# A hand-frozen instruction order laid out anew, without its zero products

## The chip, the cores and the metric

The kernel runs on one core of a Trainium2 chip. The metric is the time of one execution in microseconds (us) on the device. A core has five instruction streams that run side by side and meet only at semaphores: TensorE (PE, matrix products), VectorE (DVE), ScalarE (ACT), GpSimd (POOL) and SyncE (SP, which here issues nearly all transfers). In the profile, PEld is TensorE's loading of weights.

## The reference

Two attention blocks read the same input `x` (2048 rows of 512, bf16), with 32 heads of 16 columns each. Block A is a linear attention with a learned softmax feature map; block B is ordinary softmax attention. A gate per row mixes the two.

```python
x = A_x
g = _sigmoid((x * gate_w).sum(-1, keepdims=True))
a = _A_ref(x, A_wqkv, A_w_phi, A_wo)      # q, k through w_phi, softmax(+) and softmax(-) as features
b = _B_ref(x, B_wqkv, B_wo)               # softmax(q k^T / 4) v, 2048 x 2048 scores for each of 32 heads
return g * a + (1 - g) * b
```

The scores of block B are the bulk of the work: 32 heads x 2048 x 2048 exponentials, each of which needs a product before it and one after it.

## The kernel before, in words

**Tiles.** A score tile is 128 keys x 512 queries of one head. There are 32 blocks; a block is one chunk of 512 queries for four heads, so that a block has 4 x 16 = 64 tiles. A tile is made by one product with 32 rows of TensorE (`qk_mm`, L994: four tiles with different heads can run at once, one in each quarter of the rows), its exponential is taken, and it is used by a product with 32 columns (`pv_mm`, L1136: four at once, one in each quarter of the columns), which adds into the one accumulator `psO` of the block.

**Two ways of taking the exponential.** Most tiles go to ScalarE two at a time (`add_exp`, L1115, 128x1024). `DN` gives for each block how many tiles take the other way: VectorE writes the tile as 16-bit integers whose bits are a rough exponential (`D1`, L1084), GpSimd adds constants to the same words in two steps (`shifted`, L1060), and TensorE adds up the three versions (`add_pvd`, the operations `pvdt`, `pvds` and `pvdm`). Two D1 of the same group of four can be joined into one VectorE instruction over two banks (`Plan.join`, L1074, 128x1024). 756 tiles go this way.

**Banks.** PSUM has eight banks of 512 floats. One is `psO`; the others (`psS`, numbers 0 to 6) take the score tiles (two neighbouring banks for a ScalarE pair, one for a D1 tile) and the results of all projections. A bank that an operation takes must first have been read out by whoever drained its last content.

**Everything else fills in.** The projections of q, k and v (`k_fill`, `q_fill`, `v_fill`, `v_pair`; L754, L842, L855), the whole of block A (`phi`, `kv_half`, `z_rest`, `q_rest`) and the output products (`out_tile`, `out_part`, `out_last`) are cut into short operations (`fill`) that lie between the score products. The normalization of a finished block goes through DRAM: `ev` copies `psO` (L1231), and transfers `ld`, `lq`, `mg`, `lr`, `rb` on SP carry sums and reciprocals about, until `T2` multiplies (L1247). The odd heads of a q chunk are cut out by transfers `qo` and `qe` (L897, L899).

**The order is a table.** `_build` lists 5,401 operations with their dependencies. `Plan.place` (L477) then reads `TABLE`: for each of the five engines the list of operation numbers in the order in which its stream runs them, in `pairs` the D1 that are joined, and in `homes` one digit for each operation that takes a bank (7 is `psO`). `Plan.emit` writes the streams with the semaphore waits that the dependencies need. An engine runs its list strictly in order: an operation that waits holds up everything behind it on that engine. A `-1` in TensorE's list is a filler (`Plan.filler`, L455): four products of a block of zeros with 512 columns of `xT` (`zero_mm`, L1126), added into `psO`, where they change nothing. The numbers in the constants above the table (`DN`, `PHASES`, `POOL_ADDS`, `SHIFT` and so on) fix which tiles go which way.

```python
self.order = {e: [known[k] if k >= 0 else self.filler(k) for k in table[e]] for e in ENGINES}
for op in self.order["pe"]:
    if op.acq is not None:
        op.acq.bank = homes[int(next(bank))]
for a, k in table["pairs"]:
    self.join(known[a], known[k])
```

Of the kernel before, what the change touches and what calls it, by code (L numbers as in the profile page):

```python
# [84 lines left out]
        0, 17, 2, 4, 5, 6, 7, 8, 10, 9, 11, 13, 14, 12, 15, 22, 26, 23, 27, 24, 25, 28, 29, 21, 132, 19, 967, 133, 968, 30, 20, 1094,  # L85
        1096, 1095, 1098, 139, 1099, 140, 146, 1235, 1236, 1227, 1228, 147, 1366, 1367, 1370, 1368, 1371, 1507, 1516, 1508, 1517, 1654,
        1656, 1655, 1658, 1659, 1795, 1804, 1805, 1925, 1796, 1926, 1927, 1929, 1930, 2070, 2071, 2062, 2217, 2063, 2218, 2221, 2222,
        2219, 2358, 2349, 2350, 2359, 2484, 2485, 2486, 2488, 2489, 2625, 2634, 2635, 2626, 2763, 2764, 2765, 2767, 2768, 2900, 2891,
        2901, 531, 2892, 533, 3038, 3039, 3040, 3042, 3043, 552, 32, 554, 558, 559, 3207, 555, 562, 561, 3208, 3216, 560, 31, 557, 3346,
        3347, 3348, 556, 3350, 3217, 3351, 3483, 3491, 603, 3484, 571, 574, 605, 3492, 580, 577, 3626, 3628, 3627, 581, 584, 583, 3630,  # L90
        582, 3631, 626, 624, 3803, 3811, 627, 628, 630, 633, 634, 631, 3804, 632, 3812, 3942, 629, 3943, 3946, 3642, 3944, 3652, 3947,
        4091, 675, 4100, 3662, 4101, 4092, 677, 643, 4234, 4236, 4235, 646, 649, 4238, 652, 4239, 654, 656, 696, 698, 655, 653, 4412, 704,
        699, 4403, 702, 4404, 700, 4413, 703, 705, 4542, 4543, 701, 4546, 4544, 4547, 4260, 749, 3672, 706, 747, 4708, 4709, 4270, 715,
        718, 4250, 721, 724, 4832, 727, 4833, 726, 725, 728, 4836, 4834, 4837, 770, 768, 4280, 776, 772, 777, 775, 773, 774, 5008, 771,
        4848, 778, 5009, 5139, 5140, 787, 790, 5143, 5141, 5144, 796, 793, 800, 798, 4858, 799, 4878, 797, 4868, 5396, 5399, 5400
    ),
    "act": (
        1, 16, 3, 18, 75, 87, 81, 805, 809, 910, 806, 911, 810, 918, 916, 913, 921, 933, 923, 926, 928, 931, 938, 936, 941, 943, 948, 946,
        961, 956, 953, 951, 963, 958, 971, 969, 1058, 1065, 1053, 1050, 1060, 1048, 1068, 1055, 1063, 1073, 1078, 1075, 1080, 1083, 1070,
        1088, 1085, 1171, 1101, 1090, 1186, 1103, 1178, 1176, 1188, 1173, 1191, 1181, 1183, 1196, 1193, 1201, 1203, 1198, 1208, 1211,  # L100
        1213, 1216, 1206, 1221, 1223, 1218, 1237, 255, 1239, 1320, 260, 1325, 1322, 1327, 1330, 1332, 1335, 1337, 1340, 1342, 1345, 1347,
        1350, 1352, 1355, 1357, 282, 1360, 1362, 1374, 1376, 1466, 1468, 1471, 1473, 1476, 1478, 1481, 1483, 1486, 1488, 1491, 1493, 1496,
        1498, 1501, 1503, 1509, 1518, 1608, 287, 1610, 1613, 1615, 309, 1620, 1618, 1623, 1625, 1628, 1630, 1633, 1635, 1638, 1640, 1643,
        1645, 314, 1648, 1650, 1662, 336, 1664, 1754, 1756, 1759, 1761, 1764, 1766, 1769, 1771, 1774, 1776, 240, 1779, 1781, 1784, 1786,
        1789, 1791, 341, 1797, 1806, 1874, 1876, 1879, 1881, 1884, 1886, 1889, 1891, 1894, 1896, 1899, 1901, 1904, 1906, 1909, 1911, 1914,
        1916, 1919, 1921, 1932, 1934, 2011, 2013, 2016, 2018, 2021, 2023, 2026, 2028, 2031, 2033, 2036, 2038, 2041, 2043, 2046, 2048,
        2051, 2053, 2056, 2058, 2092, 2094, 2171, 2173, 2176, 2178, 2181, 381, 2183, 386, 2186, 2188, 2191, 2193, 2196, 2198, 2201, 2203,
        2206, 2208, 2211, 2213, 2224, 2226, 2303, 2305, 2308, 2310, 2313, 408, 2315, 2318, 413, 2320, 2323, 2325, 435, 2328, 2330, 2333,
        2335, 2338, 2340, 2343, 440, 2345, 2351, 2360, 2428, 2430, 2433, 2435, 2438, 2440, 462, 2443, 2445, 2448, 2450, 2453, 2455, 2458,
        2460, 2463, 2465, 2468, 2470, 2473, 2475, 467, 2480, 2478, 2492, 2494, 2584, 2586, 517, 2589, 2591, 2594, 2596, 2599, 2601, 2604,  # L110
        2606, 2609, 2611, 2614, 2616, 2619, 2621, 2627, 2636, 2717, 2719, 2722, 2724, 2729, 2727, 2734, 2732, 2737, 2739, 2742, 2744,
        2747, 2749, 2752, 2754, 2757, 2759, 2770, 2772, 2840, 2842, 2845, 2847, 2850, 2852, 2855, 2857, 2860, 2862, 2865, 2867, 2870,
# [1550 lines left out]
```

## Time and profile before

| | |
|---|---|
| time, median of 3 runs | 660.23 us (659.39 to 660.83) |
| span of the profiled execution, first to last instruction | 657.6 us |
| busy: TensorE products / ScalarE / VectorE / GpSimd | 649.1 / 635.1 / 609.4 / 410.8 us |
| granted TensorE clock, mean | 1.000 |
| transfers, mean | 47 GB/s |

The profiled execution's own time is not given apart from the runs; its span leaves out what lies before the first and after the last instruction, and is 2.6 us less than the median. A row of a view names the line of the kernel, the engine, the operation, what it writes and reads, how often, and then busy time, mean duration in ns, and idle time of the engine before it. Line numbers are those of helpers, so that a line can stand for many operations. A product is shown with its passage through the array (some 0.38 us), and products overlap: TensorE can look busy through a short wait. The same holds for ScalarE and VectorE, whose instructions overlap by a tenth of a microsecond.

### The profile page before, as it was taken

The numbers are of one execution on the slowest core, as the hardware profiler recorded it, in microseconds if no ns is written. First come the engines' busy times: TensorE is split into PE (matmuls) and PEld (weight loads), VectorE is DVE, ScalarE is ACT, GpSimd is POOL, SyncE is SP. The second block draws the span as 40 slices with busy tenths as digits, with TensorE's granted clock in tenths as the row PEclk, the third lists the DMA queues.
The fourth block names the chain that finished last, engine by engine and source line by source line (L and its number), as shares of the span: only waits on it lengthen the run. The fifth ranks groups of instructions, "written<-read, shape, count | busy, mean of one in ns | idle before, by whom it ended". The sixth has DMA issues, their size and how long they took to land.

```text
span 657.6 us, 20651 instructions
## 1 busy us (share of the span) xinstructions
PE 649.1 (99%) x8820; PEld 227.3 (35%) x8820; DVE 609.4 (93%) x963; ACT 635.1 (97%) x720; POOL 410.8 (62%) x437
## 2 busy tenths in 40 slices
PE   8999999999999999999999999999999999999997
PEld 4333333434333333333233233322333333332333
DVE  6999899999998789999999999999999989999985
ACT  6999999999999999999999999999989999999996
POOL 7575367465665446486467876575867566656853
PEclk9999999999999999999999999999999999999999
DMA  6530101001010000000012431233211633134132
GB/s 131 104 100 12 33 12 27 11 11 19 11 27 10 16 18 8 19 17 14 23 37 47 100 77 33 63 78 68 48 51 35 102 56 83 35 63 103 44 84 48
DMA packets 67947, 30.94 MB, mean 47 GB/s; under 512 B 53208, under 2 KB 62808, under 8 KB 67856
## 3 DMA queue, kind: packets, MB, share of 16 engines
q1 hardware_dynamic: 65840, 28.82, 19.6%
q8 instruction: 69, 1.13, 0.7%
q10 hardware_dynamic: 1632, 0.79, 0.5%
q14 instruction: 22, 0.18, 0.1%
q0 software_dynamic: 384, 0.02, 0.1%
HBM read 7.87 MB, written 8.88 MB: 25 GB/s over the span
## 4 chain that ended last, share of the span: by engine, by line
PE 85%; DVE 12%; ACT 1%; issue 1%; DMA 1%; SPq 0%; DVEq 0%
PE psO L1136 32%; PE psS L994 30%; PE psS L754 15%; DVE Tx_t L1084 3%; PE psS L1417 3%; DVE Ty_t L1084 1%; DVE oT_t L1084 1%; DVE Wp_t L1084 1%; PE psS L842 1%; ACT E_t L1115 1%; DVE Tz_t L1084 1%; PE psS L1514 1%; PE psS L855 1%; PE psO L1126 1%; DMA phiK_t<-in_A_x_dram 1%
## 5 line engine op out<-in xcount | busy, mean ns | idle before, releaser
L1115 ACT ACTIVATE E_t<-psS 128x1024 bf16<-128x1024 f32 x643 | 601.9, 1068 | 11.2 <-PE psS L994 10.3
L994 PE MATMUL psS<-qz_t,kTB_t 32*128 32x512 bf16 (+1 forms) x2054 | 267.5, 383 | 2.8 <-ACT E_t L1104 0.6
L1084 DVE TENSOR_SCALAR Tx_t<-psS 128x512 int16<-128x512 f32 x246 | 163.2, 682 | 10.5 <-PE psS L994 9.4
L994 PEld LDWEIGHTS psS<-qz_t,kTB_t 32*128 32x128 bf16 x2054 | 71.8, 91 | 226.4 <-ACT E_t L1115 102.9
L1136 PE MATMUL psO<-E_t,vaug_t 128*32 128x512 bf16 x1292 | 119.0, 384 | 0.0
L1060 POOL INT64_ADD vA_t<-vA_t x72 | 71.6, 999 | 19.0 <-PE psO L1136 13.7
L1084 DVE TENSOR_SCALAR Ty_t<-psS 128x512 int16<-128x512 f32 x114 | 76.5, 682 | 4.8 <-PE psS L994 4.5
L1060 POOL INT64_ADD Ty_t<-Ty_t x42 | 44.0, 1048 | 18.5 <-PE psO L1136 18.1
L1060 POOL INT64_ADD Ty_t<-Tx_t x29 | 30.1, 1038 | 39.0 <-DVE Tx_t L1084 32.7
L1136 PE MATMUL psO<-vA_t,vaug_t 128*32 128x512 bf16 (+1 forms) x520 | 52.6, 384 | 0.0
L1136 PE MATMUL psO<-Ty_t,vaug_t 128*32 128x512 bf16 x440 | 45.4, 384 | 0.0
L1136 PEld LDWEIGHTS psO<-E_t,vaug_t 128*32 128x32 bf16 x1292 | 30.2, 95 | 39.5 <-issue 28.4
L1084 DVE TENSOR_SCALAR oT_t<-psS 128x512 int16<-128x512 f32 x62 | 41.7, 682 | 1.5 <-PE psS L994 1.0
L1084 DVE TENSOR_SCALAR Tz_t<-psS 128x512 int16<-128x512 f32 x60 | 40.2, 680 | 2.1 <-PE psS L994 1.8
L1060 POOL INT64_ADD vA_t<-Tx_t x22 | 22.7, 1032 | 31.0 <-DVE Tx_t L1084 24.1
L1060 POOL INT64_ADD phiQT_t<-Tx_t x19 | 18.9, 993 | 29.1 <-DVE Tx_t L1084 28.0
L1084 DVE TENSOR_SCALAR vA_t<-psS 128x512 int16<-128x512 f32 x54 | 36.2, 682 | 0.7 <-PE psS L994 0.3
L1084 DVE TENSOR_SCALAR WAT_t<-psS 128x512 int16<-128x512 f32 x52 | 35.2, 682 | 1.4 <-PE psS L994 1.2
L754 PE MATMUL psS<-Wp_t,xT_t 128*32 128x512 bf16 x512 | 35.8, 382 | 0.0
L754 PE MATMUL psS<-xT_t,WB_t 128*32 128x512 bf16 x480 | 34.9, 382 | 0.2
L1084 DVE TENSOR_SCALAR Wp_t<-psS 128x512 int16<-128x512 f32 x50 | 33.8, 683 | 0.9 <-PE psS L994 0.7
L1060 POOL INT64_ADD WoB_t<-oT_t x19 | 19.3, 1016 | 20.7 <-DVE oT_t L1084 16.5
(165 smaller groups left out, 920.1 us busy)
## 6 DMA issues: line engine op xcount, KB each, us to landing
dpq<-EA_t SPq DMA_DIRECT2D x16, 256.0 KB, 2.3
Rb_t<-lr SPq DMA_DIRECT2D x120, 32.0 KB, 1.9
dpo<-kv_t SPq DMA_DIRECT2D x16, 128.0 KB, 1.8
qz_t<-qz_t SPq DMA_DIRECT2D x120, 16.0 KB, 1.8
Tf_t<-Tf_t SPq DMA_DIRECT2D x60, 32.0 KB, 2.0
WB_t<-in_B_wqkv_dram SPq DMA_DIRECT2D x3, 384.0 KB, 3.6
out_dram<-WvA_t SPq DMA_DIRECT2D x8, 128.0 KB, 2.0
out_dram<-WB_t SPq DMA_DIRECT2D x6, 128.0 KB, 2.0
```

The lines of the kernel that those rows point to most:

```text
L754: ins = e.matmul(out[32 * i:32 * i + 32, :], lhsT=lhsT[:, 32 * i:32 * i + 32], rhs=rhs, start=start, stop=stop, tile_position=(0, 32 * i))
L842: mms = [lambda e, ap, i=i, t=t: e.matmul(ap[:, 128 * i:128 * (i + 1)], lhsT=xT[:, t, NQ * c + 128 * i:NQ * c + 128 * (i + 1)], rhs=W_B[:, ...
L855: mms = [lambda e, ap, i=i, t=t: e.matmul(ap[:, 256 * i:256 * (i + 1)], lhsT=xT[:, t, NQ * c + 128 * (2 * hf + i):NQ * c + 128 * (2 * hf + ...
L994: return e.matmul(bank, lhsT=kT_B[32 * i:32 * i + 32, ROW[b // 2] % 2, 128 * kt:128 * (kt + 1)], rhs=qz[32 * i:32 * i + 32, b // 2 % 4, b ...
L1060: op = P.add("pool", P64 + W64 * size, d_prio(g["ts"][0]) - 5.0 + (0.0 if key == "s" else M_LATE), lambda e: e.int64_add(words(dst), words ...
L1084: ops.append(drain(f, mm, "dve", 0.70, d_prio(d), lambda e, ap, q=q: e.tensor_scalar(quarter(tb, q).bitcast(I16), ap, EXPB, 0.0, op0=ALU.a ...
L1115: op = P.add("act", EXP_OVH + 0.4267 * n, 0.0, lambda e: e.activation(Ebuf[:, j // 2 % EPAIRS, 512 * SZ[0] * (j % 2):512 * SZ[0] * (j % 2) ...
L1126: ins = e.matmul((psO if bank is None else bank)[32 * i:32 * i + 32, :], lhsT=zero[:], rhs=xT[:, 0, 0:NQ], start=bank is not None, stop=ba ...
L1136: return e.matmul(psO[32 * i:32 * i + w, :], lhsT=vaug[:, kt, o:o + w], rhs=rhs, start=start, stop=stop, tile_position=(0, 32 * i), skip_g ...
L1417: mms = [lambda e, ap, n=n, f=f: e.matmul(ap[:, 64 * n:64 * n + 64].rearrange("p (s g j) -> p s g j", s=2, j=4), lhsT=ident[:], rhs=es[n][ ...
L1514: mms = [lambda e, ap, g=g: e.matmul(ap[:, 64 * g:64 * g + 64], lhsT=qT(g)[:, 128 * j:128 * (j + 1)], rhs=kzbd[:, g, 0:64], start=True, st ...
```

## The change

Only `TABLE` differs. All 5,401 operations, their dependencies, the constants and so the split of tiles between ScalarE and VectorE are the same. What differs:

- **TensorE**: the 23 entries `-1` are gone (3,017 entries become 2,994). Of the others, 2,421 stand at another place, 3.9 places away in the mean and 42 at most.
- **VectorE**: 42 joined pairs in place of 59, of which 17 are in both lists; so 980 instructions in place of 963. The rest keeps nearly its order (beyond what the longer list moves).
- **ScalarE**: one operation (240, the gate's sigmoid) stands 17 places later, and a few neighbouring exponentials are exchanged.
- **GpSimd**: 300 of 433 operations stand at another place, by 1.3 places in the mean and 10 at most.
- **SyncE**: 172 of 259 stand at another place, 1.7 in the mean and 14 at most; an example is in the diff's first lines.
- **Banks**: all `homes` are dealt anew (1,575 digits, as before).

```diff
     "sp": (
-        0, 17, 2, 4, 5, 6, 7, 8, 10, 9, 11, 13, 14, 12, 15, 22, 26, 23, 27, 24, 25, 28, 29, 21, 132, 19, 967, 133, 968, 30, 20, 1094,
+        0, 17, 2, 4, 5, 6, 7, 8, 10, 9, 11, 13, 14, 12, 15, 22, 26, 23, 27, 24, 25, 28, 29, 21, 132, 133, 30, 19, 20, 967, 968,
...
     "act": (
-        1645, 314, 1648, 1650, 1662, 336, 1664, 1754, 1756, 1759, 1761, 1764, 1766, 1769, 1771, 1774, 1776, 240, 1779, 1781, 1784, 1786,
+        1771, 1774, 1776, 1779, 1781, 1784, 1786, 1789, 1791, 341, 1797, 1806, 1874, 1876, 1879, 1881, 1884, 1886, 1889, 1891, 240,
...
     "pe": (
-        813, 228, 229, 817, 917, 102, 832, 826, 929, 103, 104, 105, 919, 815, 828, 819, 922, 812, 915, 920, -1, 924, 830, 927, 869, 107,
...
     "pairs": (
-        (820, 816), (833, 827), (840, 844), (877, 879), (895, 893), (899, 897), (1010, 1012), (1032, 1030), (1035, 1037), (1129, 1127),
+        (820, 816), (827, 833), (840, 844), (877, 879), (895, 893), (897, 899), (1028, 1026), (1282, 1280), (1591, 1597),
...
     "homes": (
-        "6705645027467514305342074350243502534104260164320524035135602350263510365015430143620420342604261461024510346013546026140264052310"
+        "6705645027467531405473024352034502534104260164320524035135602350236510653103451053620352035413046163460134620342060456201462405230"
```

In the first line of SP, 132 and 133 are `qo0.1` and `qe0.1`, 30, 19 and 20 are the loads `wva`, `wbq` and `wbk`, and 967 and 968 are `ld0` and `lq0`.

More of the change, by code (lines that the diff above doesn't have):

```diff
@@ new lines @@
+        "0625605642062035650263264204056250241605026405204562406254026562300562406240256045260546250426546205604265024326054206524602540652"
+        "0465204254065236025406234260425604250645250462054260546254052640526045426504260542506250456240265405256062305623064520652042564056"
+        "2405260524506524053260542504205402654205624526405264502362053642054624504205632064205326502456042650230542054260456205462045264056"
+        "2406524066250462540256352063056245064205642605236023406436025303652356042605246504250642065260456205423052364036452604526045326034"
@@ new lines @@
+        "5024523065320534032640246042034601436204520652406254065260265065240425040246504206542642064560245406254065240524056230562304635042"
+        "3016254032506240542065240624560523065240623605420652404625046425046254062450642062302632030652406245606230536205263056420542045260"
+        "5426502645064250625460426412054625046236032063240654206351524062540526540260456230256420456240562054625042640625640254024650326502"
+        "3560452605240625405240625045205426054260240654206524650264056240625406205624503260542065246025604652405256042056250465206520625460"
@@ L363 @@
+        "524602055243502"
     ),
```

15 lines of the change are left out of this document (3 added, 12 removed), and 507 rows, old and new, of the table TABLE.

## The prediction

> **What bounds the kernel now.** I read the page first: busy times, clock and the chain that ended last.
>
> ```profile
> span 657.6 us, 20651 instructions
> PE 649.1 (99%) x8820; PEld 227.3 (35%) x8820; DVE 609.4 (93%) x963; ACT 635.1 (97%) x720; POOL 410.8 (62%) x437
> PEclk9999999999999999999999999999999999999999
> PE 85%; DVE 12%; ACT 1%; issue 1%; DMA 1%; SPq 0%; DVEq 0%
> ```
>
> Three engines are nearly full, and the chain names TensorE. A busy TensorE is not yet a TensorE at its limit, so I looked next at what a product costs, in the timeline of TensorE at one zero product (L1126).
>
> ```profile
> 408.37 0.40 PE L1136 MATMUL psO<-vA_t,vaug_t 128*32 128x512 bf16 x4
> 408.60 0.39 PE L1136 MATMUL psO<-E_t,vaug_t 128*32 128x512 bf16 x4
> 408.82 0.39 PE L1126 MATMUL psO<-xT_t,zero_t 128*32 128x512 bf16 x4
> 409.14 0.39 PE L994 MATMUL psS<-qz_t,kTB_t 32*128 32x512 bf16 x3
> ```
>
> Four products in four quarters start 0.22 us after the four before them, although each is shown with 0.39; where the quarters change from columns to rows it is 0.32, so 0.10 for the change. I walked both orders with these two prices (and sizes in proportion for narrower products). The order before needs 623.6 us, of which the 23 zero products are 6.2: 0.22 each, and ten changes that they cause. About 34 us of the span are thus TensorE waiting, most of it inside "busy". The view of waits says for whom:
>
> ```profile
> PEld psS L994 <- ACT E_t L1115: 102.9, 258, 0.6
> ACT E_t L1115 <- PE psS L994: 10.3, 27, 0.8
> ```
>
> Weight loads for score products wait for ScalarE to free a bank 258 times (0.6 us at most), ScalarE for a score product 27 times. So I read ScalarE's groups and its timeline in a full stretch.
>
> ```profile
> L1115 ACT ACTIVATE E_t<-psS 128x1024 bf16<-128x1024 f32 x643 | 601.9, 1068 | 11.2 <-PE psS L994 10.3
> 369.88 11.10 ACT L1115 ACTIVATE E_t<-psS 128x1024 bf16<-128x1024 f32 x12
> 380.72 1.24 ACT L1410 ACTIVATE EA_t<-psS 128x512 bf16<-128x512 f32 x2
> 381.68 2.11 ACT L1115 ACTIVATE E_t<-psS 128x1024 bf16<-128x1024 f32 x2
> ```
>
> From 369.88 to 380.72, 12 exponentials follow each other in 10.84 us: 0.903 each back to back (the 1.068 overlaps). The pair L1410 takes 381.68 - 380.72 = 0.96. ScalarE's least work is thus 643 x 0.903 = 581 plus 32 pairs x 0.96 = 31, so 612 of the 641 us between its first and last exponentials:
>
> ```profile
> 7.63 3.07 ACT L1104 ACTIVATE E_t<-psS 128x512 bf16<-128x512 f32 x6 [0.38 <-PE psS L994]
> L1115 ACT ACTIVATE E_t<-psS x643: 1018/1052/1299, 11.3 to 648.9; 128x1024 bf16<-128x1024 f32 x161
> ```
>
> (648.9 - 7.63 = 641; 3 us of it are the six half tiles.) ScalarE has some 26 us of slack, less than TensorE's. I take ScalarE as the engine that sets the pace, with TensorE close behind. Where the slack lies, the windows show (columns: TensorE, weight loads, VectorE, ScalarE, GpSimd):
>
> ```profile
> 132.00:165.00 33.00, 32.80 (x477) 13.31 (x465) 31.81 (x48) 31.80 (x38) 19.55 (x24) 1.00 0.08 15
> 264.00:297.00 33.00, 32.83 (x445) 11.58 (x443) 32.62 (x50) 31.53 (x35) 22.19 (x23) 1.00 0.09 19
> 297.00:330.00 33.00, 32.20 (x424) 10.88 (x421) 32.88 (x55) 32.61 (x38) 19.16 (x19) 1.00 0.08 19
> 363.00:396.00 33.00, 33.00 (x435) 10.32 (x431) 31.96 (x51) 33.00 (x39) 25.69 (x27) 1.00 0.40 80
> 396.00:429.00 33.00, 32.88 (x461) 12.10 (x457) 32.13 (x52) 33.00 (x39) 19.35 (x20) 1.00 0.18 51
> 462.00:495.00 33.00, 32.87 (x468) 11.81 (x467) 31.80 (x52) 31.13 (x38) 24.42 (x26) 1.00 0.17 47
> 528.00:561.00 33.00, 32.87 (x461) 10.90 (x453) 30.91 (x50) 31.19 (x36) 21.70 (x22) 1.00 0.28 65
> ```
>
> ScalarE is idle by 1.2, 1.5, 1.9 and 1.8 us in four of them and not at all from 363 to 429. From 264 to 330 VectorE is the full engine: 65.5 of 66 us.
>
> **The zero products.** Their own view, and the stretch that holds most of them:
>
> ```profile
> L1126 PE MATMUL psO<-xT_t,zero_t x92: 379/379/390, 17.2 to 595.9; 128*32 128x512 bf16 x92
> busy tenths in 40 slices 0110000000010000000000223430002000012000
> 361.70:444.00 82.30, 5.76 (x56) 1.47 (x56) 1.00 0.30 70
> L1115 ACT ACTIVATE E_t<-psS 128x1024 bf16<-128x1024 f32 x86 | 80.2, 1082 | 0.0
> L1410 ACT ACTIVATE EA_t<-psS 128x512 bf16<-128x512 f32 x8 | 4.8, 708 | 0.0
> ```
>
> The 92 products are 23 groups of four; 56 of them, 14 groups, lie in slices 22 to 26 of 16.4 us, from 361.7 to 444. There ScalarE runs 86 exponentials and 4 pairs with no idle time: 86 x 0.903 + 4 x 0.96 = 81.5 of 82.3 us. Without the zero products TensorE arrives at the same waits sooner; what hides the removal is ScalarE, and the stretch can give back 0.8 us at most, 0 at least. I take **-0.4**. If that cover were gone, 14 x 0.22 to 0.32 would be worth 3.1 to 4.5. In the four windows where ScalarE is idle there are none (slices 8 to 9, 16 to 17, 28 to 29 and 32 to 33 have the digit 0). The other nine can give 0 to 9 x 0.32 = 2.9; a score product that starts sooner helps only if its exponential was late, and outside the four windows few were. I take a third, **-0.9**.
>
> **The joined pairs.** 17 more VectorE instructions net:
>
> ```profile
> L1084 DVE TENSOR_SCALAR Tx_t<-psS 128x512 int16<-128x512 f32 x246 | 163.2, 682 | 10.5 <-PE psS L994 9.4
> L1074 DVE TENSOR_SCALAR Tx_t<-psS 128x1024 int16<-128x1024 f32 x21 | 25.6, 1221 | 1.5 <-PE psS L994 1.5
> ```
>
> Two single ones take 2 x 0.682 = 1.364, a joined one 1.221: 0.14 more each, 2.4 in all. VectorE has 657.6 - 609.4 = 48 us to spare, which hides it everywhere but from 264 to 330, where the pairs before were six and the tiles of the new list's pairs ran as five: one split more. A split also frees its first bank half a microsecond sooner. Bounds 0 and +2.4; I take **+0.2**.
>
> **TensorE's order.** The new one needs 617.7 us by the same walk, 5.9 less; the old one without zero products 617.4. There are 1,218 changes of form for 1,215, against 5 fewer rounds of score products: new order and old are equally dense. No gain from packing, **0**, between -0.6 and +0.3.
>
> **The transfers.** Nothing of before is late by a landing: the normalization's two VectorE steps behind them waited for none.
>
> ```profile
> L1240 DVE RECIPROCAL rd_t<-Lq_t 128x32 f32<-128x32 f32 x15 | 5.1, 339 | 0.0
> L1247 DVE TENSOR_TENSOR oT_t<-Tf_t,Rb_t 128x512 bf16<-128x512 f32 x15 | 10.7, 716 | 0.0
> SPq L899 <- DMA qz_t<-qz_t: 7.2, 7, 1.3
> 41.29 0.51 SPq L689 DMA_DIRECT2D WB_t<-in_B_wqkv_dram  x1
> ```
>
> So an allowance for late landings has nothing to win here. What it can lose is on SP: `qe0.1` now stands ahead of `wva`, `wbq` and `wbk`, and while it waits for the landing of `qo0.1` (such waits are 1.3 us at most) the three loads stand behind it, and the k and q projections of row 1 behind these. The last of the loads goes out at 41.3 now, and the first product that reads it stands at 51.2 us of product time in the old list and 51.0 in the new, with all waits still to be added: that distance hides it. Without it the price is 1.3. **0**, up to +1.3.
>
> **The banks.** This is the unknown. A bank can't come back sooner than a score product and its reader last: 0.383 + 1.068 = 1.45 us for an exponential, 0.383 + 0.682 = 1.07 for a single D1, 0.383 + 1.221 = 1.60 for a joined one (0.383 is the row of L994):
>
> ```profile
> L994 PE MATMUL psS<-qz_t,kTB_t 32*128 32x512 bf16 (+1 forms) x2054 | 267.5, 383 | 2.8 <-ACT E_t L1104 0.6 <-DVE Tx_t L1074 0.4 <-DVE Tx_t L1084 0.4
> ```
>
> Along each order I counted the takings of a bank that come closer, in product time, to its last taking than that. Before: 26, short by 4.4 us in all. Before with the zero products struck out: 43, short by 8.7. New: 47, short by 11.2. Each is a sure wait of TensorE, though neighbouring ones overlap. From 4.4 to 8.7 is what the zero products covered, and is in the terms above. The other 2.5 are the new order's own. Bounds 0 and +2.5; I take a third, **+0.8**, since most sure waits fall where ScalarE is full anyway.
>
> **Sum.** -0.4 - 0.9 + 0.2 + 0 + 0 + 0.8 = -0.3 us. The span becomes 657.3, and with the 2.6 us by which the median of the runs exceeds the span the forecast is 659.9, which I call no change: less than 0.2% (1.3 us) can't be told from none with this kernel.
>
> **Rival 1, faster: the new order closes ScalarE's gaps.** A new deal of order and banks can bring score products sooner where ScalarE is idle. The four windows hold 1.2 + 1.5 + 1.9 + 1.8 = 6.4 us; half of that, with the zero products' 1.3, is 4.5 under the median: **655.7**. For it: 26 us of slack are there to be found. Against it: the new order is no denser, and the windows from 264 to 330 are VectorE's, whose work does not shrink.
>
> **Rival 2, slower: tight banks in the middle.** Of the new order's sure waits, 8.3 us fall between 264 and 429 us of product time (before 1.9; before without zero products 4.4). VectorE is full in the first third of that stretch and ScalarE in the rest, so neither can catch up. If the growth of 6.4 us reaches ScalarE, less a third by which neighbours overlap (a guess), it is 4.3 over the median: **664.5**. It decides once ScalarE falls under 33.00 busy between 363 and 429. Against it: ScalarE's wait for L994 is only 10.3 us now, so most waits of TensorE do not reach it.
>
> **Rival 3: the zero products cost their full price.** If TensorE alone were the bound, as the chain's 85% reads, all 5.9 us would come off: **654.3**. Against it: the weight loads' 102.9 us behind ScalarE.
>
> **Rival 4: the clock.** The clock row is full throughout, and the longest wait in the view of waits is 0.6 us. If it fell to half for one slice of 16.4 us, that slice's products would take as long again: **677**. The Trainium skill, "TensorE: Matmul & The Clock Gate", section "A second HAM failure mode: psum-queue depth-cycling", says that short idle times between groups of products while banks cycle can make the clock swing between half and full, which speaks against taking filler work out. By that rule, the trace does not bear it out: the 34 us of waits are there already, at full clock.
>
> **How the numbers follow.** No change as summed 40%, rival 1 31%, rival 2 26%, rival 3 2%, rival 4 1%. The likeliest case alone, by its bounds (-0.8 - 2.9 - 0.6 to +2.4 + 0.3 + 1.3 + 2.5), could reach 655.9 to 666.7; since the terms will not all fall on one side I give it 657.5 to 662.5; of its 40 points 8 lie below 658.9, 27 between that and 661.5, and 5 above. Faster is 8 + 31 + 2 = 41%, the same 27%, slower 5 + 26 + 1 = 32%. The range, 655.0 to 665.0, takes in rivals 1 and 2 at their prices and leaves out 3, 4 and the tails.
>
> **What would show it.** Right: no row of L1126; TensorE's busy time still near its span; ScalarE at 33.00 from 363 to 429 with some 39 instructions in each window, as now; the weight loads' wait for L1115 up by 2 to 5 us; VectorE x980, busy 611 to 612. Rival 1: the idle time ahead of L1115 falls from 11.2 to 7 or less. Rival 2: it rises over 15, between 264 and 429. A landing that shows as idle time ahead of L1240 or L1247, or among the waits of TensorE, would prove my zero for the transfers wrong; a digit under 9 in the clock row, the one for the clock.

## The result: slower by 0.9%

The kernel after takes 666.05 us (median of 4 runs, 665.17 to 666.67) beside 660.45 us of the kernel before on the same chip (659.39 to 660.83): a ratio of 1.009, 95% interval 1.0078 to 1.0102. The forecast was 659.9 us, no change; the range ended at 665.0. The page of the kernel after, the rows that answer to those shown of before:

```profile
span 664.1 us, 20458 instructions
PE 652.5 (98%) x8728; PEld 231.2 (35%) x8728; DVE 612.3 (92%) x980; ACT 637.2 (96%) x720; POOL 411.1 (62%) x437
PEclk9999999999999999999999998999999999999999
...
L1127 ACT ACTIVATE E_t<-psS 128x1024 bf16<-128x1024 f32 x643 | 603.0, 1058 | 13.0 <-PE psS L1006 11.3
```

All lines stand 12 lower than before (L1115 is now L1127, L994 L1006, L1084 L1096, L1444 L1456). The zero products are gone, VectorE has 980 instructions, and the span is 6.5 us longer. One digit of the clock row is 8: the slice from 398 to 415 us. The waits hardly differ in sum:

```profile
PEld psS L1006 <- ACT E_t L1127: 101.2, 259, 0.9
ACT E_t L1127 <- PE psS L1006: 11.3, 27, 1.1
```

The windows (columns: TensorE, weight loads, VectorE, ScalarE, GpSimd, clock) say where it went. ScalarE, which ran without idle time from 363 to 429 before, no longer does:

```profile
363.00:396.00 33.00, 32.41 (x418) 10.12 (x421) 32.05 (x53) 32.86 (x38) 25.40 (x26) 1.00 0.34 83
396.00:429.00 33.00, 32.30 (x412) 11.07 (x404) 30.53 (x49) 31.71 (x37) 21.16 (x22) 0.95 0.14 42
429.00:462.00 33.00, 31.45 (x376) 9.62 (x372) 31.31 (x50) 32.34 (x36) 19.08 (x20) 1.00 0.23 62
```

The sharpest ruler is the start of the same exponential in two traces. ScalarE's list is the same but for a few neighbours, so that the lag of one kernel behind another shows each loss at its place. The lags behind the kernel before, in us (columns are runs told below; "new" is the kernel after):

| exponential (its start before) | new | e1 | f1 | f2 | f4 |
|---|---|---|---|---|---|
| first, 7.6 us | 1.08 | 0.04 | 0.11 | 0.21 | 0.04 |
| 16.9 | 1.23 | 0.04 | 0.02 | 0.13 | 0.04 |
| 355.1 | 1.33 | -0.21 | -0.08 | 0.01 | -0.26 |
| 366.2 | 2.24 | -0.32 | 0.05 | 0.14 | -0.37 |
| 389.9 | 2.46 | -0.21 | 0.20 | 0.29 | -0.26 |
| 412.3 | 3.88 | 0.84 | 1.66 | 0.92 | -0.50 |
| 447.4 | 4.94 | 0.66 | 1.89 | 1.35 | -0.69 |
| 593.0 | 5.92 | 0.65 | 2.03 | 1.79 | -0.75 |
| last, 648.9 | 5.26 | 0.52 | 1.36 | 1.13 | -0.88 |
| end of the span, 657.6 | 6.45 | 0.52 | 2.54 | 2.32 | -0.89 |

The last row but one is the last start in the rows of the exponentials' line (before: 648.9), here of new, f1, e1 and f4:

```profile
L1127 ACT ACTIVATE E_t<-psS x643: 1018/1042/1202, 12.7 to 654.1; 128x1024 bf16<-128x1024 f32 x161
```

```profile
L1136 ACT ACTIVATE E_t<-psS x643: 1017/1042/1194, 11.4 to 650.2; 128x1024 bf16<-128x1024 f32 x161
```

```profile
L1135 ACT ACTIVATE E_t<-psS x643: 1018/1069/1319, 11.4 to 649.4; 128x1024 bf16<-128x1024 f32 x161
```

```profile
L1135 ACT ACTIVATE E_t<-psS x643: 1017/1064/1318, 11.4 to 648.0; 128x1024 bf16<-128x1024 f32 x161
```

The new kernel's lag jumps at three places: at 355 to 366, at 390 to 412, and at 436 to 447. Another 1.2 us come behind the last exponential: from its start to the end of the span it is 8.8 us before and 10.0 in the kernel after.

### The profile page after: what moved, and what is told of

Same layout as the page of the kernel before. It is cut to its first block, busy times and chain, and to the rows that moved or that the text cites. A ratio compares the mean times of both kernels' runs of the same rounds, so it can differ in the third digit from the quotient of the medians.

```text
span 664.1 us, 20458 instructions
## 1 busy us (share of the span) xinstructions
PE 652.5 (98%) x8728; PEld 231.2 (35%) x8728; DVE 612.3 (92%) x980; ACT 637.2 (96%) x720; POOL 411.1 (62%) x437
## 5 line engine op out<-in xcount | busy, mean ns | idle before, releaser
L1127 ACT ACTIVATE E_t<-psS 128x1024 bf16<-128x1024 f32 x643 | 603.0, 1058 | 13.0 <-PE psS L1006 11.3
L1006 PE MATMUL psS<-qz_t,kTB_t 32*128 32x512 bf16 (+1 forms) x2054 | 271.2, 384 | 4.9 <-DVE Tx_t L1096 1.1
L1096 DVE TENSOR_SCALAR Tx_t<-psS 128x512 int16<-128x512 f32 x252 | 166.9, 682 | 9.0 <-PE psS L1006 8.2
L1006 PEld LDWEIGHTS psS<-qz_t,kTB_t 32*128 32x128 bf16 x2054 | 73.6, 91 | 224.3 <-ACT E_t L1127 101.2
L1148 PE MATMUL psO<-E_t,vaug_t 128*32 128x512 bf16 (+1 forms) x1292 | 123.0, 385 | 0.6 <-DVE Tf_t L1243 0.3
L1096 DVE TENSOR_SCALAR Ty_t<-psS 128x512 int16<-128x512 f32 x116 | 77.8, 683 | 3.8 <-PE psS L1006 3.5
L1096 DVE TENSOR_SCALAR oT_t<-psS 128x512 int16<-128x512 f32 x70 | 47.0, 684 | 4.3 <-PE psS L1006 3.9
L1148 PEld LDWEIGHTS psO<-E_t,vaug_t 128*32 128x32 bf16 (+1 forms) x1292 | 32.2, 95 | 45.9 <-issue 32.4
L1096 DVE TENSOR_SCALAR Tz_t<-psS 128x512 int16<-128x512 f32 x62 | 41.5, 682 | 2.7 <-PE psS L1006 2.3
L1096 DVE TENSOR_SCALAR WAT_t<-psS 128x512 int16<-128x512 f32 x58 | 39.3, 685 | 2.7 <-PE psS L1006 2.6
L1072 POOL INT64_ADD oT_t<-Ty_t x19 | 18.0, 948 | 35.8 <-DVE Ty_t L1096 35.7
L1096 DVE TENSOR_SCALAR vA_t<-psS 128x512 int16<-128x512 f32 x58 | 38.7, 683 | 0.8 <-PE psS L1006 0.7
L1096 DVE TENSOR_SCALAR Wp_t<-psS 128x512 int16<-128x512 f32 x56 | 37.7, 683 | 0.8 <-PE psS L1006 0.6
L1148 PE MATMUL psO<-Tx_t,vaug_t 128*32 128x512 bf16 (+1 forms) x288 | 29.7, 384 | 0.0
```

Source lines behind the costliest of these rows:

```text
L1006: return e.matmul(bank, lhsT=kT_B[32 * i:32 * i + 32, ROW[b // 2] % 2, 128 * kt:128 * (kt + 1)], rhs=qz[32 * i:32 * i + 32, b // 2 % 4, b ...
L1072: op = P.add("pool", P64 + W64 * size, d_prio(g["ts"][0]) - 5.0 + (0.0 if key == "s" else M_LATE), lambda e: e.int64_add(words(dst), words ...
L1096: ops.append(drain(f, mm, "dve", 0.70, d_prio(d), lambda e, ap, q=q: e.tensor_scalar(quarter(tb, q).bitcast(I16), ap, EXPB, 0.0, op0=ALU.a ...
L1127: op = P.add("act", EXP_OVH + 0.4267 * n, 0.0, lambda e: e.activation(Ebuf[:, j // 2 % EPAIRS, 512 * SZ[0] * (j % 2):512 * SZ[0] * (j % 2) ...
L1148: return e.matmul(psO[32 * i:32 * i + w, :], lhsT=vaug[:, kt, o:o + w], rhs=rhs, start=start, stop=stop, tile_position=(0, 32 * i), skip_g ...
```

## The experiments

Each time is a median, each ratio is to the kernel before on the same chip with its 95% interval. Theory C blames the clock, O the new order's bank waits, and F says that zero products cost their full time; the other theories are told where they are first tried. Traces, and with them the lags, are of one execution of each kernel; of the other executions the time and the mean granted clock are on record. A mean of 0.997 belongs to one stretch of 3.41 us at half clock, 0.995 to two (6.83 us in the trace of e3).

**The zero products alone, out of the old order and into the new one.** Run e1 strikes the 23 fillers out of the table before, run e2 puts 23 into the new one. TensorE's list at one of the 23 places each, e1 against before and e2 against after:

```diff
-922, 812, 915, 920, -1, 924, 830, 927,
+922, 812, 915, 920, 924, 830, 927,
```

```diff
-3222, 3221, 3316, 3252, 3250, 3299,
+3222, 3221, 3316, -1, 3252, 3250, 3299,
```

> The order before with its 23 zero products struck out and nothing else changed. Theory C (the zero products hold the clock; without them a window of 3.4 us falls to half clock, as at 402 us in the changed kernel, and costs up to 1.7 us each time): a half-clock stretch shows, mean clock under 1.000, 661.5 to 664. Theory O (the new order's bank waits are the loss, and the zero products only filled waits): clock 1.000 and 659.0 to 661.2, no change. Theory F (the zero products cost their full 6 us): 654 to 656.

> The new order with the 23 zero products put back, each ahead of the operation that it preceded in the order before (three of them moved a few places, out of the hand-over of psO). Theory C: clock 1.000 throughout and 660.5 to 662.5, most of the 5.6 us back. Theory O: 664.5 to 667, whatever the clock does, since the waits for banks between 360 and 450 us remain.

e1: 659.94 us, ratio 0.9991 (0.9979 to 1.0002). e2: 671.65 us, ratio 1.0185 (1.0154 to 1.0216). Taking the zero products out of the old order changes nothing that can be measured, so the loss is not theirs. Putting them into the new one adds 5.6 us, more than any of the theories expected. Three of e2's six executions have the full clock, the profiled one among them, and they take 670.4 to 671.0 us: C cannot be the main cause. (By the prediction's walk of TensorE's list they add 9.6 us of product time there, as they also part neighbours that run side by side; in the old order 6.2.) In the profiled execution of e1 two forces cancel. Its lag falls to -0.45 us at 401 us and is +0.84 at 412, because the clock falls to half for one stretch of 3.41 us:

```profile
397.03:400.45 3.42, 3.23 (x55) 1.54 (x58) 3.38 (x7) 3.42 (x5) 1.99 (x2) 1.00 0.02 5
400.45:403.86 3.41, 3.41 (x32) 1.08 (x30) 2.16 (x5) 2.35 (x3) 0.44 (x1) 0.50 0.01 2
```

Here 32 products and 3 exponentials run where 55 and 5 did in the stretch ahead of it; the column behind GpSimd's is the granted clock. Four of e1's eleven executions have such a stretch by their mean clock; they took 660.0 us in the mean, the other seven 659.3.

**Which half of the order.** Run e3 has the old order, zero products included, up to 356 us and the new one behind it; run e4 is its mirror. All five lists, the pairs (51 and 50) and the banks are cut at that time; e3 keeps 4 of the zero products, e4 19. Against the kernel after, e3 differs at the lists' beginnings (here the pairs) and e4 at their ends (here TensorE's):

```diff
-        (820, 816), (827, 833), (840, 844), (877, 879), (895, 893), (897, 899), (1028, 1026),
+        (820, 816), (833, 827), (840, 844), (877, 879), (895, 893), (899, 897), (1010, 1012),
```

```diff
-5375, 5391, 5376, 5377, 5378, 5379, 5380, 5381
+5391, 5377, 5378, 5394, 5397, 5379, 5380, 5381
```

> The order before (4 of its zero products) for everything that began by 356 us, then the new order without zero products. Both theories put the loss behind 360 us: 664 to 666.5, with a half-clock stretch near 400. If a good part of the loss lies ahead of 356 us (the two traces differ by 1.1 us from the first exponential on), 661 to 663.5.

> The new order to 356 us, then the order before with its 19 zero products. Both theories: 660 to 661.5, no change against before, clock 1.000. If the part ahead of 356 us costs something, 661.5 to 664.

e3: 666.52 us, ratio 1.0089 (1.0068 to 1.011), as slow as the whole new order. e4: 661.15 us, ratio 1.0016 (1.0005 to 1.0028). Nearly all of the loss arises behind 356 us. (Of e4's 2.0 us in its trace 0.8 are there at the first exponential; 1.0 come between 355 and 366 us, at the cut.)

**What happens at the jumps.** I then compared the length of the same VectorE instruction in both traces. They agree but for a handful, and those that are longer in the new kernel are all of one kind: multiplications with both inputs in SBUF. `phi0.x.1` multiplies half of a feature tile of block A by a ratio, and `rt0.x` makes that ratio. First the kernel after (minimum, median, maximum in ns):

```profile
L1456 DVE TENSOR_TENSOR EA_t<-EA_t,ratio_t x16: 680/690/1525, 338.1 to 604.2; 128x512 bf16<-128x512 bf16 x16
...
L1439 DVE TENSOR_TENSOR ratio_t<-ratio_t,statq_t x8: 215/215/1054, 337.9 to 590.0; 128x64 f32<-128x64 f32 x8
...
L1096 DVE TENSOR_SCALAR Tx_t<-psS x252: 623/682/694, 14.7 to 643.0; 128x512 int16<-128x512 f32 x126
```

And the kernel before:

```profile
L1444 DVE TENSOR_TENSOR EA_t<-EA_t,ratio_t x16: 675/682/707, 335.4 to 594.0; 128x512 bf16<-128x512 bf16 x16
```

Three of the sixteen `phi0.x.1` (at 338.7, 359.7 and 439.8 us) take 1.52, 1.53 and 1.51 us in place of 0.69, and one of the eight `rt0.x` (at 590.0) 1.05 in place of 0.22. The 252 instructions of the last row, which read PSUM, never exceed 0.694. The kernel before has long ones of its own, at other places: `T2.1` (1.20 in place of 0.68), `g1` (0.82 for 0.17), `kz0` (1.05 for 0.68) and `tb30` (0.93 for 0.73), 1.7 us in all; all but `g1`, which reads one tile of SBUF, are such multiplications too. The first of the places in the kernel after, VectorE and then GpSimd:

```profile
337.87 0.21 DVE L1439 TENSOR_TENSOR ratio_t<-ratio_t,statq_t 128x64 f32<-128x64 f32 x1
338.12 2.13 DVE L1456 TENSOR_TENSOR EA_t<-EA_t,ratio_t 128x512 bf16<-128x512 bf16 x2
340.18 0.68 DVE L833 CAST kTB_t<-psS 128x512 bf16<-128x512 f32 x1
```

```profile
338.41 1.30 POOL L1072 INT64_ADD WoB_t<-WoB_t  x1 [0.95 <-PE psO L1148]
```

A GpSimd add gets its data at 338.3 us, while the first multiplication runs. It waits for it, and takes 1.30 us in place of 1.04 for that reason; then it runs until 339.71, and the second multiplication, though next on VectorE, ends only at 340.25, 0.54 later. In the old order a copy from PSUM stands between the two multiplications:

```profile
335.39 0.68 DVE L1444 TENSOR_TENSOR EA_t<-EA_t,ratio_t 128x512 bf16<-128x512 bf16 x1
336.00 1.27 DVE L821 CAST kTB_t<-psS 128x512 bf16<-128x512 f32 x2
337.19 0.68 DVE L1444 TENSOR_TENSOR EA_t<-EA_t,ratio_t 128x512 bf16<-128x512 bf16 x1
```

```profile
337.32 1.45 POOL L1060 INT64_ADD WoB_t<-WoB_t  x1 [0.78 <-PE psO L1136]
```

There the same add is the one that waits (1.45), and nothing of VectorE waits for it. The Trainium skill, "SBUF — State Buffer", section "Who interferes with whom", states the rule: a VectorE instruction with two SBUF inputs and a GpSimd instruction that reads SBUF use the same port; whichever comes first keeps it to its end, the other stands still. This trace agrees, in both directions, and so do the instructions on PSUM, which run on undisturbed.

**The four collisions taken away.** Run f1 is the kernel after with one wait more on each of the four GpSimd adds: it now waits for the multiplication that it used to overtake.

```diff
         known, bank = list(self.ops), iter(table["homes"])
+        for k, n in table["late"]:
+            known[k].deps = known[k].deps + [known[n]]
...
+    "late": ((2936, 532), (3085, 553), (3742, 625), (4771, 766), ),
```

> The kernel after, with four GpSimd adds made to wait for the VectorE multiplication that they delayed: the add of slice 64.93 waits for phi0.1.1, 64.98 for phi0.3.1, 64.131 for phi0.7.1, 64.178 for rt0.15. In the kernel after, these four VectorE instructions took 1.52, 1.53, 1.51 and 1.05 us where their kind takes 0.69 and 0.22. Theory P (each such stretch on VectorE is passed on to the exponentials): the four are back at 0.69 and 0.22, and the time falls by about 0.8 us for each of the three long ones, to 663.0-664.2 us, with the half-clock stretch still there. Theory O (the new order loses by bank waits all over, VectorE has slack): 665.5-666.5 us. Theory C (the half clock alone is the loss behind 356 us): 665.5-666.5 us as long as the clock still falls.

662.54 us, ratio 1.0053 (1.0036 to 1.007). The four are back at their length, and VectorE's busy time falls from 612.3 to 608.9 us:

```profile
PE 650.1 (98%) x8728; PEld 230.0 (35%) x8728; DVE 608.9 (92%) x980; ACT 635.7 (96%) x720; POOL 410.7 (62%) x437
```

```profile
L1465 DVE TENSOR_TENSOR EA_t<-EA_t,ratio_t x16: 677/684/692, 336.9 to 600.3; 128x512 bf16<-128x512 bf16 x16
...
L1448 DVE TENSOR_TENSOR ratio_t<-ratio_t,statq_t x8: 211/215/226, 336.6 to 586.8; 128x64 f32<-128x64 f32 x8
```

```profile
336.89 1.29 DVE L1465 TENSOR_TENSOR EA_t<-EA_t,ratio_t 128x512 bf16<-128x512 bf16 x2
...
338.36 1.04 POOL L1081 INT64_ADD WoB_t<-WoB_t  x1 [2.12 <-PE psS L1015]
```

The medians are 3.5 us apart, the ratios 0.37% or 2.4 us; that is a little more than P had, and in two of f1's six executions the clock stayed full, which it did in none of the four of the kernel after. The two profiled executions have one half-clock stretch each. The lag table gives 2.7: at the last exponential new stands 3.9 us behind f1, of which 1.2 is there at 16.9 us already (see the last section). Of the 3.3 us of stretched VectorE time four fifths thus go through to the end: the distance of the two columns is 1.4 at 355 us, 2.2 at 366 and 412, 3.05 at 447 and 3.9 at 593, so some 0.2 for the first collision and 0.8 for each of the others. Theory P holds; O and C as sole causes fall. The collisions are the largest part of the loss, but not all of it. (e4 has one more case, at full clock: at its cut `rt0.3` and `phi0.3.1` are 1.1 us longer than in the kernel before, and its lag grows by 1.0.)

**The same neighbourhoods put into the kernel before.** Run f3 changes VectorE's list alone, at three places (529, 550, 622 are `rt0.1`, `rt0.3`, `rt0.7`; 530, 532, 551, 553, 623, 625 the multiplications):

```diff
-2928, 529, 2988, 532, 3055, 3050, 530, 3060,
+2928, 2988, 3055, 3050, 529, 530, 532, 3060,
-3118, 550, 3156, 3149, 3151, 551, 3138, 3133, 553,
+3118, 3156, 3149, 550, 551, 553, 3151, 3138, 3133,
-3717, 623, 3735, 3746, 3741, 625, 3632, 3810, 3802, 3839,
+3717, 3735, 3746, 3741, 622, 625, 3632, 3810, 3802, 3839, 623,
```

> The kernel before, with only VectorE's list changed in three places to what the new order has there: rt0.1, phi0.0.1, phi0.1.1 back to back; rt0.3, phi0.2.1, phi0.3.1 back to back; rt0.7 and phi0.7.1 back to back with phi0.6.1 behind D1.21.10.2. All zero products stay. Theory P: the second multiplication of each takes about 1.5 us where the GpSimd add that waits gets in between, and the time rises by about 0.8 us for each that does, to 661.5-662.6 us. Theories O and C: no change beyond 0.5 us, 659.7-660.7 us.

662.00 us, ratio 1.0038 (1.0026 to 1.005): the time that P expected, but not by its working. At the first place the collision came, at the third hardly (0.82 us in place of 0.68, without a lag), and at the second the small `rt0.3` was hit instead:

```profile
337.14 2.13 DVE L1465 TENSOR_TENSOR EA_t<-EA_t,ratio_t 128x512 bf16<-128x512 bf16 x2
...
357.85 0.77 DVE L1448 TENSOR_TENSOR ratio_t<-ratio_t,statq_t 128x64 f32<-128x64 f32 x1
358.66 1.29 DVE L1465 TENSOR_TENSOR EA_t<-EA_t,ratio_t 128x512 bf16<-128x512 bf16 x2
```

The first cost 0.1 us of lag. The second cost 1.26: of these 0.55 is the stretch (0.77 in place of 0.22). The rest I put down to the two multiplications that now stand ahead of three D1 whose banks TensorE wants back; no run separates the two. So a neighbourhood on VectorE can cost more than its collision.

**The clock.** Run f2 is f1 with five zero products, ahead of the operations 3389, 3458, 3476, 3481 and 3904. Run f4 is the kernel before with four of its 23, ahead of 3389, 3458, 3476 and 3486, those between 388 and 402 us. (Of f2's five the last runs at 444 us, the others between 388 and 400.) One place of f2 against f1, and one of the 19 places of f4 against before:

```diff
-3375, 3389,
+3375, -1, 3389,
```

```diff
-922, 812, 915, 920, -1, 924,
+922, 812, 915, 920, 924,
```

> The kernel of the run before this one, with 5 of the 23 zero products put back: ahead of pvds.114, qk382, pv387.18, pv389.18 and qk437, where TensorE streams least (44.9% of the 3.41 us before the clock fell). Theory C: granted clock 1.000, no half-clock stretch, and 1.0-1.5 us less than the run before this one, after some 0.4 us for the five products themselves. Theory O: the clock is 1.000 and the time moves by under 0.5 us. With P and C both right 661.5-663.0 us; with O alone 665.5-667 us.

> The kernel before with 4 of its 23 zero products: those ahead of pvds.114, qk382, pv387.18 and Q2.2 (388 to 402 us); the other 19 left out. Theory C (the zero products there hold the clock, and without them the half-clock stretch takes back what the others' absence gives): granted clock 1.000 and 658.3-659.3 us, faster than both kernels. Theory N (zero products lie in waits and cost nothing, the clock neither): 659.6-660.4 us.

f2: 662.88 us, ratio 1.0048 (1.0036 to 1.006), as f1. f4: 658.76 us, ratio 0.9991 (0.9982 to 0.9999): at best the fastest kernel here, with e1 and g3, but by less than the 0.2% that tell from no change. Both profiled executions have the full clock, and so have all eleven of f4; of f2's five, two do not (mean clock 0.997). In f4 the stretch around 400 us reads

```profile
397.87:401.28 3.41, 3.33 (x57) 1.52 (x58) 3.38 (x8) 3.41 (x5) 2.44 (x2) 1.00 0.02 5
401.28:404.69 3.41, 3.41 (x55) 1.06 (x43) 3.41 (x6) 3.41 (x5) 1.31 (x2) 1.00 0.03 7
```

and in the kernel after

```profile
398.79:402.21 3.42, 2.99 (x50) 1.44 (x49) 3.42 (x8) 3.42 (x5) 3.22 (x3) 1.00 0.02 5
402.21:405.62 3.41, 3.41 (x30) 0.86 (x32) 3.03 (x6) 2.69 (x4) 0.00 (x0) 0.50 0.19 71
```

f4 and e1 are the same to 0.05 us up to 390 us; behind the half-clock stretch e1 stands 1.35 us further back. That is the price of one such stretch in this pair of traces, and the four fillers' use. In the new order the fillers gained 0.7 us of lag at 412 us, of which 0.2 is left at the end. C is right that the clock falls; but the old order without zero products pays for it too and still ends level with before. In the new one f2's fillers bring no time in the median, which is that of an execution where the clock fell. The executions of f1 among themselves do show a price: 661.1 and 661.2 us at full clock, 662.0 and 663.6 with one stretch by the mean clock, 663.1 and 664.9 with two. All four of the kernel after lost one or two. So the clock has a share in its loss, some 0.7 (e1) to 1.6 us (f1) a stretch by so few executions; and at full clock f1 is still 1.8 us behind the kernel before (659.38 on that chip).

**What is left.** f1 still stands 0.5% behind the kernel before. I took, for each product, its start less the product time ahead of it in the walk: TensorE's waits so far. At 420 us of product time they are 29.85 us in e1 and 29.75 in f1. By this ruler the mended new order is level with the old one there; at the end they are 37.2 and 39.1. The lag table has it otherwise: f1's exponentials stand 1.2 us behind e1's at 447 already and 0.8 at the last one, and the other 1.2 us come behind that. So theory S of the next two runs, by which what is left lies in waits spread behind 456 us, stands against R, a backlog carried there. Runs g1 and g2 cut at 456 us: g1 has f2's order first and that of before without zero products behind (47 pairs), g2 f4's first and the new one behind (54 pairs, and the one wait for `rt0.15`). The end of TensorE's list, g1 against f2 and g2 against f4:

```diff
-5375, 5391, 5376, 5377, 5378, 5379, 5380, 5381
+5391, 5377, 5378, 5394, 5397, 5379, 5380, 5381
```

```diff
-5391, 5377, 5378, 5394, 5397, 5379, 5380, 5381
+5375, 5391, 5376, 5377, 5378, 5379, 5380, 5381
+    "late": ((4771, 766), ),
```

> The new order with the four GpSimd waits and the five zero products of the run f2 up to about 456 us, and the order of before, without its zero products, behind that. TensorE's waits (start of a product less the product time ahead of it) stand at 28.4 us in f2 and 27.7 us in f4 at 456 us, and at 37.4 and 34.8 at the end. Theory S (what is left of the loss is the new order's own waits spread over the stretch behind 456 us, about 2 us): 659.0-660.4 us, waits at the end some 35.5 us. Theory R (the loss is a backlog that the new order carries into that stretch, so any order behind it ends late): 661.5-663 us.

> The mirror of the run g1: the order of before with four zero products (run f4) up to 456 us, the new order without zero products behind it, its one locked pair there (rt0.15) mended by the GpSimd wait. Theory S: the late stretch adds its 2 us, 660.2-661.4 us. Theory R: 658.5-659.5 us, as f4.

g2: 662.12 us, ratio 1.0033 (1.0021 to 1.0045), between nothing and the whole loss, and above the ranges of both theories. It can't be used for S, since most of its loss lies at the cut: behind f4, the same kernel up to 456 us, its exponentials stand 0.2 us at 456 and 2.75 at 470. ScalarE waits there for a score product, which neither f2 nor f4 has it do:

```profile
459.37 7.67 ACT L1137 ACTIVATE E_t<-psS 128x1024 bf16<-128x1024 f32 x8 [2.12 <-PE psS L1016]
```

g1 can't be used by its time either: 665.02 us, ratio 1.0084 (1.0066 to 1.0101), since the cut itself made VectorE wait for a transfer and TensorE behind it, upon which the clock fell again for 3.4 us:

```profile
469.55 0.35 DVE L1262 RECIPROCAL rd_t<-Lq_t 128x32 f32<-128x32 f32 x1 [2.37 <-DMA Lq_t<-ld]
```

Past their cuts, though, the two traces agree. From 470 us to the last exponential neither order loses anything: the lag behind the kernel before goes from 2.1 to 1.6 us in g2 (new order) and from 5.8 to 5.5 in g1 (old order). Behind the last exponential the new order costs 1.2 us: from its start to the end of the span it is 9.97 or 9.98 us in all six kernels that end in the new order (after, e2, e3, f1, f2, g2), and 8.78 to 8.80 in the eight others. The lists say what differs. Behind the last product of block 31 that uses an exponential TensorE has 17 groups of four output products to run in the old list and 22 in the new, where five that used to lie ahead of it (the last four of `OP15`, and `O13.0`) have come behind. Five times 0.22 is 1.1 us, at a time when ScalarE has no exponential left to hide it. Here is ScalarE's last reading of such a product, before and after (5.5 and 6.9 us after the start of the last exponential):

```profile
654.32 0.69 ACT L1350 ACTIVATE WB_t<-psS,gT_t 128x512 bf16<-128x512 f32 x1 [0.83 <-PE psS L754]
```

```profile
660.98 0.69 ACT L1362 ACTIVATE WB_t<-psS,gT_t 128x512 bf16<-128x512 f32 x1 [0.61 <-PE psS L766]
```

No run put the five back. Of the other 0.8 us of f1 behind e1, 0.4 are there at 366 us, 0.7 come by 456, and 0.3 are won back behind that; I did not divide them further. S is not borne out: what is left is partly R's backlog, and partly the end of the list, which neither theory had.

**The collision of before, and the transfers.** Run g3 gives f4 one wait against the longest stretch of a VectorE instruction on 128x512 in the kernel before, `T2.1` (its expectation calls it the only one; `g1`, `kz0` and `tb30` are stretched too). Run g4 is the kernel before with SP's new list and nothing else.

```diff
+    "late": ((1134, 1100), ),
```

```diff
     "sp": (
-        0, 17, 2, 4, 5, 6, 7, 8, 10, 9, 11, 13, 14, 12, 15, 22, 26, 23, 27, 24, 25, 28, 29, 21, 132, 19, 967, 133, 968, 30, 20, 1094,
+        0, 17, 2, 4, 5, 6, 7, 8, 10, 9, 11, 13, 14, 12, 15, 22, 26, 23, 27, 24, 25, 28, 29, 21, 132, 133, 30, 19, 20, 967, 968,
```

> The kernel of f4 (before with four zero products) with one GpSimd add, s64.15, made to wait for the VectorE multiplication T2.1 at 74 us, the one stretched VectorE instruction of before (1.20 us instead of 0.68). Theory P (each stretch is passed on): 0.4-0.6 us less than f4, 658.0-658.6 us. Theory V (at 74 us VectorE has slack, its stretch costs nothing): as f4, 658.5-659.3 us.

> The kernel before with only SP's list (the order in which the transfers are issued) taken from the new order; everything else, the zero products too, as before. If the order of the transfers costs nothing, as the prediction had it: 659.5-660.5 us. If transfers now land late somewhere: 660.8 us or more, with a wait of TensorE or VectorE on a transfer that is over 0.5 us longer.

g3: 658.68 us, ratio 0.9991 (0.9979 to 1.0002), as f4. The stretch is gone and nothing is won: theory V, VectorE has room at 74 us. The other three were not tried. g4: 663.58 us, ratio 1.0076 (1.0047 to 1.0104). The new order of transfers with the old lists of the others is 0.8% slower, and its `T2` shows where:

```profile
L1268 DVE TENSOR_TENSOR oT_t<-Tf_t,Rb_t x15: 673/681/1207, 75.6 to 639.1; 128x512 bf16<-128x512 f32 x15
...
  DMA Rb_t<-lr: 1.5, 1
  DMA Tf_t<-Tf_t: 0.7, 1
```

VectorE waits for two landings, 0.7 us at 366 and 1.5 at 481, and the exponentials fall back by 1.1 and 1.5 us behind them; another 1.2 us of this trace are there at the first exponential, where the clock came late (see the last section). With its own VectorE list the new order has one such wait, 1.0 us at 639, behind which no lag shows:

```profile
L1259 DVE TENSOR_TENSOR oT_t<-Tf_t,Rb_t x15: 675/682/692, 75.3 to 638.9; 128x512 bf16<-128x512 f32 x15
...
  DMA Rb_t<-lr: 1.0, 1
```

Late landings are thus a real price of the new order of transfers beside the old lists, and next to none beside the new ones.

## Why the prediction was wrong

The balance of the two profiled runs, 664.1 - 657.6 = 6.5 us: 2.7 for the collisions (new against f1), 0.5 for zero products and one half-clock stretch together (e1 against before), 2.0 for the rest of the new order (f1 against e1), of which 1.2 lie behind the last exponential and 0.8 ahead of it, and 1.2 that was there by 16.9 us, which belongs to the execution and not to the order (see the last section). By its steps:

- **What bounds the kernel.** ScalarE's pace and TensorE's closeness held. VectorE's 48 us to spare was read as cover; a mean over the span did not cover the 0.8 us that each of three collisions cost.
- **Zero products, -1.3.** Their removal won 0.45 us by 401 us in e1, and lost 1.3 behind it. f4, where the clock is kept, stands 0.88 us ahead of before at the last exponential with 19 of the 23 gone: the term without the clock was right in kind, and 1.3 somewhat high.
- **Rival 4, the clock, at 1%.** The trigger was seen and the case dismissed, with the argument that 34 us of waits are there at full clock already. The mechanism came, in every execution of the kernel after; its size was wrong too, one or two stretches of 3.41 us, and 1.35 us of time for one (e1 against f4), not a slice of 16.4. The rule of the Trainium skill that the prediction set aside ("TensorE: Matmul & The Clock Gate", section "A second HAM failure mode: psum-queue depth-cycling") is borne out in part: in the profiled executions of the four kernels without a filler around 400 us (after, e1, e3, f1) the clock fell there, and in the ten others it did not fall there. It is not strict: without a filler there e1 kept the clock in seven of eleven executions and f1 in two of six, and with fillers f2 lost it in two of five.
- **Joined pairs, +0.2.** The counts held (x980), and "busy 611 to 612" nearly did (612.3), for the wrong reason: 3.3 us of it are the stretched multiplications, and without them it is 608.9 (f1), while the 609.4 of before hold 1.7 us of stretches of their own. Two single D1 behind each other start 0.60 us apart, and what follows a joined one starts 1.14 after it: un-joining adds 0.06 us each, not 0.14.
- **TensorE's order, 0.** Nothing measured speaks against the density. But the walk counts what there is to do, and not where it stands: the five groups of products that the new list leaves for the end cost 1.2 us, which no term of the sum holds.
- **Transfers, 0.** Right for the whole table, wrong for the list by itself (g4). One landing was late by 1.0 us, within the +1.3 that the text had allowed; no lag shows behind it.
- **Banks, +0.8, and rival 2 (664.5).** The rival was 1.5 us from the time, and its sign (ScalarE under 33.00 from 363 to 429) came. But its cause was a small part at most: with the collisions mended, TensorE's waits in its stretch, up to 420 us of product time, are those of the old order without zero products, where it had the growth of 6.4 us. The idle time ahead of the exponentials is 13.0, not over 15, and the weight loads' wait for them fell by 1.7 us in place of rising by 2 to 5. Up to the last exponential the order's own loss is 0.8 us (f1 against e1), which is the +0.8 of the sum; that it is so close is luck, since nothing shows that these are its sure waits.
- **The step that failed** is the part on VectorE: the prediction costed its new list as "17 more VectorE instructions net", +0.2, and nothing else, and so took every other instruction to keep its length wherever it stands. In its place the runs showed four multiplications stretched by 3.3 us, of which 2.7 reached the end; with them mended (f1) the time is 662.54 us. The end of TensorE's list, 1.2 us, and the clock, at 1%, were left out beside it. `T2.1` at 1.200 us in the row of L1247, 0.52 over its kind, stood in the trace of before as a warning that some VectorE instructions stop for GpSimd; the prediction's own row of L1247 has a mean of 716 where the median is 681:

```profile
L1247 DVE TENSOR_TENSOR oT_t<-Tf_t,Rb_t x15: 675/681/1200, 74.4 to 635.4; 128x512 bf16<-128x512 f32 x15
```

## What to carry to other kernels

When an order is laid out anew, compare the longest instance of each instruction with its median: a maximum of twice the median in a row of equal shapes can be another engine on the same port. Two VectorE instructions with both inputs in SBUF should not stand back to back where a GpSimd instruction may become ready in between; either put work on PSUM between them or let the GpSimd instruction wait, which is the one with slack here (busy 411 of 664 us). What hides a product in the middle of a kernel is gone at its end: count what stands behind the last instruction of the engine that sets the pace. Few filler products, near the place where TensorE streams least, did as much as 23 (f4), and more than that won nothing here. And lists of different engines belong together: SP's new list alone cost 0.8% beside the old ones, and the cut order g1 was slower than both orders that it was cut from (f2 and e1).

## What the runs showed of the hardware

- **A waiting GpSimd add takes the port between two multiplications.** The second one then stands still until the add ends: 1.51 to 1.53 us in place of 0.69, in three places of the kernel after. In these it was the order of arrival that decided, and not that the second multiplication was next on VectorE.
- **Half clock without a long gap.** In the stretch ahead of the fall at 402.21 no two products start more than 0.7 us apart. Of its 50 products, 32 are only four columns wide:

```profile
398.90 0.24 PE L1513 MATMUL psS<-kzbd_t,phiQT_t 128*128 128x4 bf16 x4
```

The window for that line alone (products, weight loads, clock):

```profile
398.79:402.21 3.42, 0.85 (x32) 0.76 (x31) 1.00 0.02 5
```

That these narrow products let the clock fall was not tried by itself; f4 has 21 of them in its stretch of 3.41 us, with two fillers, and keeps its clock.
- **The start differs from run to run.** The clock's first record at full stands at 4.0 us in f1 and at 9.7 in the kernel after, with the same instructions up to there, and at 9.1 in g4; four products of 256 columns take 1.06 us in the kernel after at 6.4 us and 0.60 in f4 at 6.2. g3's profiled run got its full clock at 15.8 us: behind f4 its exponentials are 1.2 us late at the first, 3.6 at 16.9 us and 3.5 at the last, and it took 662.11 us beside its median of 658.68.

```profile
6.43 1.06 PE L880 MATMUL psS<-xT_t,WB_t 128*128 128x256 bf16 x4
```

```profile
6.18 0.60 PE L888 MATMUL psS<-xT_t,WB_t 128*128 128x256 bf16 x4
```

The 1.2 us at the start of the kernel after's profile are of this kind, and no property of its order: f1, with the same lists up to there, does not have them.
